# Two early expert tiles: tokens read in 32-token blocks and turned on VectorE, w1 loaded in block order

## The chip, the cores and the metric

One core of one Trainium2 chip runs the whole program. The metric is the device time in microseconds (us). Runs of one kernel on this chip are compared with each other, and the profile is one further execution of the same program.

## The reference

An FFT layer over the sequence is followed by a mixture of experts in which each token goes to one expert.

```python
def _attn_ref(x, w_r, w_i, b_r, b_i):             # x: 8 x 2496 x 256
    X = np.fft.rfft(x, axis=1)
    Yr = Xr @ w_r - Xi @ w_i + b_r                # 256 x 256 each
    Yi = Xr @ w_i + Xi @ w_r + b_i
    ...                                           # soft threshold at 0.01
    y = np.fft.irfft(Y, n=x.shape[1], axis=1)
def _moe_ref(x, w_gate, w1, w2):                  # 19968 tokens, 8 experts
    logits = x @ w_gate
    expert_idx = np.argmax(logits, axis=1)
    ...                                           # gate_w: softmax value of the chosen expert
    for e in range(E):
        mask = expert_idx == e
        h = np.maximum(xe @ w1[e], 0.0)           # 256 -> 1024
        ye = h @ w2[e]                            # 1024 -> 256
        out[mask] = gate_w[mask, None] * ye
```

## The kernel before

**Two phases.** The first (`spectral`) does the transforms of the eight sequences. `route` then works out for each half of a sequence, (b, 0) and (b, 1), in which row of a DRAM table `xs` each token belongs, and its `scatter` writes the tokens there, sorted by expert: up to 11 indirect DMAs a half, issued by GpSimd (POOL) on L813, 117 rows of 264 floats each. The second phase takes `xs` in tiles of 512 tokens of one expert. Tiles 0 to 2 (`EARLY` = 3) begin before the last sequence is scattered, because full tiles of the earlier sequences stand already; tile 3 and all later ones need every scatter. The last 32 scatters, of (6, 1), (7, 0) and (7, 1), run while tiles 0 and 1 are worked on.

**One tile.** `load` reads its tokens, `weights` its expert's w1 and w2. `upright` makes the token matrix with features on the partitions, as a rounded part `xh` (ScalarE, ACT) and a remainder `xl` (VectorE, DVE); `split1` and `split2` cut w1 and w2 in the same way. `up` is the first product, eight groups of six matmuls into a bank `ph`; of each group ACT makes `hh` (L1229) and DVE `hl` (L1230). `down` is the second product, four banks (128 tokens each) of 17 matmuls (L1405, L1406); product j of a bank needs `hh[j]` and `hl[j-1]`. `done` scales the result and sends it to `out` by an indirect DMA (L1269). While `down(t)` runs, its `work` makes the weights and, for tiles 1 and 2, the tokens of tile t+1; tokens of tile 3 and later are made during `up(t)`.

**Two forms of the tokens.** Tiles 0 to 2 are read as rows (`xw`, L1000, one DMA, 1056 bytes a token), and TensorE (PE) turns them by eight 128x128 transposes into `px` (L1172). Tile 3 and later are read in blocks of 32 tokens (`xq`, L1005, four DMAs of 256-byte runs, and `xr`, L1008, two words a token), and DVE turns them by two block transposes (L1148) into `xf`. That leaves the features in another order, so `by_block` loads w1 in the same order (four DMAs of 32 partitions each).

**What sets the order.** PE, SyncE (SP), ACT and DVE run their instructions as the code writes them. POOL's order is made by the compiler's scheduler until `experts_rest`. A scatter may not be moved ahead of the last `mark` copy written before it (`pace`, `gated`): tiny POOL copies (L742) of a word that another engine has just made. `up` of an early tile writes one mark for each `hh` group and two scatters behind it. Any scatter that stands behind the reads of `xs` for tiles 1 and 2 waits until those DMAs are done, since the table's rows could overlap. SP issues all loads in one queue: after the w1 of tile 3 come `xq` and `xr` of tile 3 (which wait for all scatters), the raw w1 `qb` of an expert (L1072, `read_units`; `sum_units` on POOL, L1077 to L1080, and `split_units` on ACT and DVE make a combined form of it that later tiles use), `xq` and `xr` of tile 4, and w2 of tile 3. In `down(2)` ACT and DVE work in this order: `split_units`, `split2(3)`, `split1(3)`; `up(3)` needs the last of these.

Of the kernel before, what the change touches and what calls it, by code (L numbers as in the profile page):

```python
# [10 lines left out]
F32 = mybir.dt.float32  # L11
F32R = mybir.dt.float32r
BF16 = mybir.dt.bfloat16
I32 = mybir.dt.int32
# [10 lines left out]
D = 256  # L25
E = 8
F = 1024
LAM = 0.01
XW = 264
# [8 lines left out]
EARLY = 3  # L38
# [81 lines left out]
class Kernel:  # L120
# [48 lines left out]
    def open_inverse(self, st):  # L169
        nc, nb = self.nc, self.nb  # L170
        cp = self.cp
        self.idle = cp.tile([128, 512], BF16, name="idle")
        nc.vector.memset(self.idle, 0.0)
        self.ident = cp.tile([128, 128], F32, name="ident")
        make_identity(nc, self.ident)
        self.carry = cp.tile([117, E], F32, name="carry")
        self.carry_b = cp.tile([117, E], BF16, name="carry_b")
        self.base = cp.tile([128, E], F32, name="base")
        nc.vector.memset(self.carry, 0.0)
        nc.vector.memset(self.carry_b, 0.0)  # L180
        self.ones_b = cp.tile([117, 128], BF16, name="ones_b")
        nc.vector.memset(self.ones_b, 1.0)
        self.used = cp.tile([128, E], F32, name="used")
        nc.vector.memset(self.used, 0.0)
        self.tabs = [cp.tile([4, 128], I32, name=f"tab{i}") for i in range(4)]
        cp.tile([1, 384 * (len(self.tabs))], I32, name="gap")
        self.drop = cp.tile([128, 128, 2], I32, name="drop")
        self.tcol = cp.tile([128, 6], F32, name="tcol")

        k = self.k = self.pool(st, "k", 1)  # L190
        self.wi = self.pool(st, "wi", 3)
        self.rt = self.pool(st, "rt", 1)
        self.psi = self.pool(st, "psi", 2, space=PSUM)
        self.iw = k.tile([128, 2, 136], F32, name="iw")
        self.gar = k.tile([120, 117], F32, name="gar")
        self.gh = k.tile([120, 117], F32R, name="gh")
        self.gl = k.tile([120, 117], F32R, name="gl")
        self.ids = k.tile([117, nb, G], I32, name="ids")
        self.score = k.tile([117, G, E], F32, name="score")
        self.ltri_f = k.tile([117, 117], F32, name="ltri_f")  # L200
        self.ltri = k.tile([117, 117], BF16, name="ltri")
        self.scan = [k.tile([117, 8 + GH, E], F32, name=f"scan{i}") for i in range(3)]
        for t in self.scan:
            nc.vector.memset(t[:, 0:8, :], 0.0)
        self.mark = k.tile([1, 1], F32, name="mark")
        self.z = k.tile([128, 2, 66, 40], F32, name="z")
# [780 lines left out]
    def load(self, t):  # L987
        if t >= self.nt or t in self.seen:
            return
        self.seen.add(t)  # L990
        nc = self.nc
        n = self.length(t)
        row = self.word(2, t, E * self.cap + 2 * TT - n)
        rows = self.xs[bass.ds(row, n), :]
        if t < self.early:
            if t:
                xr = self.w2p.tile([128, 4, XW], F32, tag="xw", name="xw", bufs=EARLY - 1)
            else:
                xr = self.rt.tile([128, 4, XW], F32, name="xw0")
            nc.sync.dma_start(xr, rows.rearrange("(h p) c -> p h c", h=4))  # L1000
            self.xfs[t], self.xrs[t] = xr, xr[:, :, HEAD:HEAD + 2]
            return
        xq = self.hb.tile([128, 16, 2, 32], F32, tag="xq", name="xq", bufs=2)[:, :n // 32]
        for q in range(4):
            nc.sync.dma_start(xq[32 * q:32 * q + 32].rearrange("p t c i -> p t (c i)"),  # L1005
                              rows[:, 64 * q + q // 2 * E:64 * q + q // 2 * E + 64].rearrange("(t j) c -> j t c", t=n // 32))
        xr = self.hb.tile([128, 4, 2], F32, tag="xr", name="xr", bufs=7)
        nc.sync.dma_start(xr[:, :n // 128, :], rows[:, HEAD:HEAD + 2].rearrange("(h p) c -> p h c", h=n // 128))  # L1008
        self.xqs[t], self.xrs[t] = xq, xr

    def weights(self, t, which):
        if t >= self.nt:
            return
        nc = self.nc
        e = self.word(0, t, E - 1)
        back = 2 if self.wide < t < self.main else 1
        ask = {} if t > self.wide and t - back < self.wide or t == self.main else self.unless_kept(t, back)
        raw1, raw2 = self.raws(t)
        if which == 2:
            parts = [(raw2[q], self.w2[bass.ds(e, 1), q * 512:(q + 1) * 512, :].rearrange("o (c p) f -> p (o c) f", p=128))  # L1020
                     for q in range(2)]
        elif t < self.early:
            parts = [(raw1[:, q], self.w1[bass.ds(e, 1), q * 128:(q + 1) * 128, :].rearrange("o p f -> p (o f)"))
                     for q in range(2)]
        else:
            parts = [(raw1[at], src) for at, src in self.by_block(bass.ds(e, 1))]
        for dst, src in parts:
            nc.sync.dma_start(dst, src, **ask)
# [107 lines left out]
        self.next_weights(t, 2)  # L1136

    def turn_tokens(self, t):
        if t >= self.nt or t < self.early or t in self.xfs:
            return  # L1140
        nc = self.nc
        n = self.length(t)
        xf = self.xf.rearrange("p (c t j) -> p c t j", c=2, t=16)[:, :, :n // 32, :]
        self.xfs[t] = [xf[:, c].rearrange("p t j -> p (t j)") for c in range(2)]
        xq = self.xqs.pop(t)
        for lo in range(0, n // 32, 8):
            hi = min(lo + 8, n // 32)
            nc.vector.transpose(xf[:, :, lo:hi, :].rearrange("p c t j -> p t c j"), xq[:, lo:hi])  # L1148
            yield
# [12 lines left out]
    def upright(self, t):  # L1162
        if t >= self.nt:
            return
        nc = self.nc
        n = self.length(t)
        if t < self.early:
            xf = []
            for c in range(2):
                p = self.psi.tile([128, 512], F32, tag="u", name="px", bufs=4)  # L1170
                for h in range(4):
                    nc.tensor.transpose(p[:, h * 128:(h + 1) * 128], self.xfs[t][:, h, c * 136:c * 136 + 128],  # L1172
                                        self.ident)
                xf.append(p)
        else:
            yield from self.turn_tokens(t)
            xf = self.xfs.pop(t)
        if self.fewer(t) or self.home(t) is self.w2p:
            xh, xl = (self.w2p.tile([128, 2, 2 * TT], F32R, tag=nm, name=nm)[:, :, :n] for nm in ("xh2", "xl2"))
        else:  # L1180
            xh, xl = (self.alt[:, i:i + 4 * TT].rearrange("p (c n) -> p c n", c=2)[:, :, :n] for i in (0, 4 * TT))
        if self.fewer(t):
            sums = self.xsum
            th, tl = self.xss[t] = [self.alt[:, i:i + 3 * TT] for i in (0, 3 * TT)]
        for c in (1, 0) if self.fewer(t) else (0, 1):
            with self.tc.high_priority():
                nc.scalar.copy(xh[:, c], xf[c])
            with self.tc.high_priority():
                nc.vector.tensor_sub(xl[:, c], xf[c], xh[:, c])
            yield  # L1190
        if self.fewer(t):
            nc.scalar.copy(th, sums)
            nc.vector.tensor_sub(tl, sums, th)
            yield
        self.xts[t] = (xh, xl)
# [327 lines left out]
    def experts_rest(self, late):  # L1523
        late.enter_context(self.tc.manual_schedule(engines={mybir.EngineType.Activation, mybir.EngineType.DVE, mybir.EngineType.Pool}))
        self.hb = self.pool(late, "hb", 1)
        self.rt = self.pool(late, "rt2", 1)
        self.xf = self.hb.tile([128, F], F32, name="xf")
        self.xsum = self.hb.tile([128, 3 * TT], F32, name="xsum")
        self.alt = self.hb.tile([128, 8 * TT], F32R, name="alt")
        self.five = self.hb.tile([128, 2 * TT], F32, name="five")  # L1530
# [55 lines left out]
```

## Time and profile before

| what | value |
|---|---|
| median of 3 runs | 1457.04 us (1456.46 to 1457.08) |
| the profiled execution: time | 1456.64 us |
| the profiled execution: span of the core | 1454.8 us |
| busy share PE / DVE / ACT / POOL | 99% / 77% / 67% / 47% |

The span runs from the core's first to its last instruction; 1.8 us of the profiled execution lie outside it. All times below count from the start of the span. Tiles 0 to 3 take up about 563 to 655 us of it.

### The profile page before, as it was taken

What the parts mean: (1) busy time and instruction counts of PE and PEld (TensorE: products, weight loads), DVE (VectorE), ACT (ScalarE), POOL (GpSimd) and SP (SyncE); (2) the same over time, 40 slices, a digit from 0 to 9 for tenths busy, and PEclk for the clock granted to TensorE, in tenths of its full rate; (3) what the DMA queues carried; (4) which work ended last, traced back from release to release, by engine and by line L of the source; (5) the groups of instructions that cost most, each with busy time, mean ns of one, the idle gap of its engine ahead of it and who ended that gap; (6) DMA issues with size and microseconds to landing.
All of it is one profiled execution on the core that took longest, in us unless ns stands there. A gap on an engine that the chain in (4) does not pass through costs nothing.

```text
span 1454.8 us, 30914 instructions
## 1 busy us (share of the span) xinstructions
PE 1436.6 (99%) x9989; PEld 1307.9 (90%) x9990; DVE 1113.5 (77%) x2475; ACT 972.3 (67%) x2054; POOL 683.2 (47%) x791
## 2 busy tenths in 40 slices
PE   9999999999999999999999999999999999999997
PEld 8898989898999988888888899999999999999996
DVE  5778787878888988787787677777777777777785
ACT  5767767677676666566665666666676677666664
POOL 2113342516161536654544566565656655665521
PEclk9999999999999999999999999999999999999999
DMA  7665464646463225699698674273283392751482
GB/s 225 179 203 156 142 189 122 194 122 193 117 191 98 82 90 183 148 250 270 180 242 232 180 213 111 59 233 84 59 254 70 73 241 72 206 129 45 126 239 62
DMA packets 200701, 227.89 MB, mean 157 GB/s; under 512 B 115735, under 2 KB 162213, under 8 KB 195412
## 3 DMA queue, kind: packets, MB, share of 16 engines
q1 hardware_dynamic: 180166, 179.37, 46.3%
q0 software_dynamic: 20144, 46.38, 10.1%
q8 instruction: 81, 1.33, 0.4%
q14 instruction: 89, 0.72, 0.2%
q10 hardware_dynamic: 221, 0.09, 0.0%
HBM read 221.32 MB, written 80.72 MB: 208 GB/s over the span
## 4 chain that ended last, share of the span: by engine, by line
PE 87%; DVE 6%; issue 3%; ACT 2%; POOL 1%; SPq 0%; DMA 0%; DVEq 0%; POOLq 0%; ACTq 0%
PE po L1406 15%; PE pd L1297 10%; PE ph L1225 8%; PE ph L1297 8%; PE po L1405 8%; PE pm L457 6%; PE pz L548 5%; PE pd L1406 5%; PE pb L424 4%; PE pa L381 4%; PE py L562 4%; PE pk L457 3%; PE pv L528 3%; PE pd L1405 2%; DVE y L518 2%
## 5 line engine op out<-in xcount | busy, mean ns | idle before, releaser
L1406 PE MATMUL po<-h,hh 128*128 128x512 f32 x928 | 326.2, 395 | 0.0
L1405 PE MATMUL po<-h,hl 128*128 128x256 f32 x928 | 241.3, 280 | 0.0
L1269 POOL DMA_INDIRECT out<-o,row x80 | 116.7, 1459 | 246.3 <-DVE o L1267 178.4
L813 POOL DMA_INDIRECT xs_dram<-yb,pos x171 | 173.5, 1014 | 62.4 <-issue 31.4
L1406 PEld LDWEIGHTS po<-h,hh 128*128 128x128 f32 x928 | 168.8, 188 | 27.1
L1405 PEld LDWEIGHTS po<-h,hl 128*128 128x128 f32 x928 | 175.0, 189 | 8.7
L518 DVE SCALAR_TENSOR_TENSOR y<-v,r 64x256 f32<-64x256 f32 x320 | 134.0, 419 | 6.4 <-ACT r L505 0.8
L1135 POOL TENSOR_TENSOR h<-r,h 128x512 fp32r<-128x512 f32 x108 | 136.6, 1301 | 0.4
L1406 PE MATMUL pd<-h,hh 128*128 128x512 f32 x368 | 127.8, 394 | 0.0
L1269 POOL DMA_INDIRECT out<-o,xr x70 | 70.8, 1011 | 119.0 <-DVE o L1267 87.4
L742 POOL COPY mark<-v 1x1 f32<-1x1 f32 x70 | 13.7, 196 | 216.1 <-DVE v L491 192.2
L1267 DVE SCALAR_TENSOR_TENSOR o<-po,xr,part 128x256 f32<-128x256 f32 x108 | 51.8, 480 | 82.2 <-ACT part L1266 82.1
L1337 ACT ACTIVATE hh<-pd 128x512 fp32r<-128x512 f32 x108 | 64.6, 598 | 73.3 <-DVE ph L1332 61.3
L1229 ACT ACTIVATE hh<-ph 128x512 fp32r<-128x512 f32 x108 | 64.5, 598 | 69.8 <-PE ph L1225 68.5
L1106 DVE TENSOR_TENSOR l<-r,h 128x512 fp32r<-128x512 f32 x164 | 105.6, 685 | 2.8 <-ACT h L1105 2.2
L1230 DVE SCALAR_TENSOR_TENSOR hl<-ph,hh 128x512 fp32r<-128x512 f32 x108 | 74.1, 689 | 41.7 <-ACT hh L1229 39.2
L1342 DVE SCALAR_TENSOR_TENSOR hl<-pd,hh 128x512 fp32r<-128x512 f32 x108 | 74.6, 691 | 38.4 <-ACT hh L1337 34.4
L1405 PE MATMUL pd<-h,hl 128*128 128x256 f32 x368 | 95.6, 280 | 0.0
L1297 PE MATMUL pd<-alt,qb 128*128 128x256 f32 x648 | 93.6, 280 | 0.8 <-DVE pd L1328 0.8
L548 PE MATMUL pz<-iw,z 128*120 128x136 f32 x684 | 93.6, 279 | 0.3 <-ACT z L532 0.3
L1105 ACT CAST h<-r 128x512 fp32r<-128x512 f32 x164 | 92.9, 617 | 0.0
L528 PEld LDWEIGHTS pv<-bi,y 128*128 128x128 f32 x640 | 79.8, 192 | 13.8 <-issue 7.3
(261 smaller groups left out, 4544.4 us busy)
## 6 DMA issues: line engine op xcount, KB each, us to landing
qb<-pw_dram SPq DMA_DIRECT2D x54, 1024.0 KB
r<-moe_w SPq DMA_DIRECT2D x88, 512.0 KB
r<-moe_w SPq DMA_DIRECT2D x152, 256.0 KB
spec_dram<-ae SPq DMA_DIRECT2D x77, 240.0 KB
t<-spec_dram SPq DMA_DIRECT2D x140, 128.0 KB
xq<-xs_dram SPq DMA_DIRECT2D x140, 128.0 KB
pw_dram<-qb SPq DMA_DIRECT2D x16, 1024.0 KB
x<-x SPq DMA_DIRECT2D x35, 384.0 KB
```

The source lines that it names most:

```text
L457: nc.tensor.matmul(to, a[:, c, slot, :], ww[nm][:, c, :], start=first and i == 0, stop=last and i == 5, skip_group_check=held)
L518: self.nc.vector.scalar_tensor_tensor(out=y[q * 64:q * 64 + 64, kp, :], in0=u[h, q, :], scalar=LAM, in1=r[h, q, :], op0=ALU.add, op1=ALU.min)
L528: nc.tensor.matmul(p[:, c, :, kp, :], y[:, kp, c * 128:(c + 1) * 128], self.bi[:, 2 * s + kp, :], start=True, stop=True)
L548: nc.tensor.matmul(p[:120, c * 128:c * 128 + 136], self.z[:, c, 3 * g:3 * g + 3, :].rearrange("p j a -> p (j a)"), self.iw[:, c, :], start ...
L813: i = nc.gpsimd.indirect_dma_start(out=self.xs[:, :], out_offset=bass.IndirectOffsetOnAxis(ap=pos[:m, g:g + 1], axis=0), in_=y[:m, g, 0:XW ...
L1106: nc.vector.tensor_sub(lo[:, c, s], v, hi[:, c, s])
L1135: self.nc.gpsimd.tensor_sub(lo[:, s, :], self.r2[q // 2][:, q % 2 * 2:q % 2 * 2 + 2, :], hi[:, s, :])
L1225: nc.tensor.matmul(p[:, i, :], a, v[:, c, :], start=m == 0, stop=m == 5)
L1269: i = nc.gpsimd.indirect_dma_start(out=self.out[:, :], out_offset=bass.IndirectOffsetOnAxis(ap=at[h], axis=0), in_=o[:, h, :], in_offset=N ...
L1297: nc.tensor.matmul(to[:, k * TT:k * TT + TT], w, v, start=start and k == m == 0, stop=m == 2, skip_group_check=True)
L1405: nc.tensor.matmul(p[:, :D], hl[:, f, hs], w2[:, f, 0, :], start=False, stop=False)
L1406: nc.tensor.matmul(p, hh[:, j, hs], w2[:, j].rearrange("p a d -> p (a d)"), start=j == 0, stop=j == 7)
```

## The change

Tiles 1 and 2 are read, turned and multiplied as the later tiles are: five DMAs instead of one for the tokens, two DVE block transposes instead of eight PE transposes, w1 in the order of blocks. Tile 0 keeps its old form. The load of w1 of tile 1 loses its condition. The turned tokens `xf` move to a pool that lives from the start, into what had been an unused gap; nothing else in memory moves.

```diff
-        cp.tile([1, 384 * (len(self.tabs))], I32, name="gap")
+        self.xf = cp.tile([128, F], F32, name="xf")
+        cp.tile([1, 384 * (len(self.tabs)) - F], I32, name="gap")
...
-        if t < self.early:
-            if t:
-                xr = self.w2p.tile([128, 4, XW], F32, tag="xw", name="xw", bufs=EARLY - 1)
-            else:
-                xr = self.rt.tile([128, 4, XW], F32, name="xw0")
+        if t == 0:
+            xr = self.rt.tile([128, 4, XW], F32, name="xw0")
             nc.sync.dma_start(xr, rows.rearrange("(h p) c -> p h c", h=4))
...
-        xq = self.hb.tile([128, 16, 2, 32], F32, tag="xq", name="xq", bufs=2)[:, :n // 32]
+        if t < self.early:
+            both = self.w2p.tile([128, 4 * XW], F32, tag="xw", name="xw", bufs=EARLY - 1)
+            xq = both[:, :4 * D].rearrange("p (t c i) -> p t c i", t=16, c=2)
+            xr = both[:, 4 * D:4 * D + 8].rearrange("p (h c) -> p h c", h=4)
+        else:
...
-        ask = {} if t > self.wide and ... else self.unless_kept(t, back)
+        ask = {} if t == which == 1 or t > self.wide and ... else self.unless_kept(t, back)
...
-        elif t < self.early:
+        elif t == 0:
             parts = [(raw1[:, q], self.w1[bass.ds(e, 1), q * 128:(q + 1) * 128, :].rearrange("o p f -> p (o f)"))
...
-        if t >= self.nt or t < self.early or t in self.xfs:
+        if t >= self.nt or t == 0 or t in self.xfs:
...
-        if t < self.early:
+        if t == 0:
             xf = []
```

The order of instructions moves on POOL, about the last 32 scatters. The rows begin where sequence 7 ends (the marks on `y` and `yb`) and tile 0 starts; `xs_dram<-yb,pos` is a scatter, `mark<-hh` a mark on a group of tile 0's `up`, `out<-o` a result of tile 0. Before:

```order
L742 COPY mark<-y 1x1
L742 COPY mark<-yb 1x1
L813 DMA xs_dram<-yb,pos 162304x264 x11
L742 COPY mark<-hh 1x1
L813 DMA xs_dram<-yb,pos 162304x264 x2
...
L742 COPY mark<-hh 1x1
L813 DMA xs_dram<-yb,pos 162304x264 x2
L1269 DMA out<-o,xw_7790 19968x256
L813 DMA xs_dram<-yb,pos 162304x264 x4
```

Now:

```order
L743 COPY mark<-y 1x1
L743 COPY mark<-yb 1x1
L743 COPY mark<-hh 1x1 x6
L814 DMA xs_dram<-yb,pos 162304x264 x23
L1272 DMA out<-o,xw_7791 19968x256
L814 DMA xs_dram<-yb,pos 162304x264 x4
```

Before, eleven scatters stood ahead of the first mark on `hh`, and two behind each of the six marks; now all six marks stand ahead of all 23 scatters. The sixth mark reads group 5 of tile 0's `up`. Behind these rows the order is the same in both: the result DMAs of tile 0 among the last nine scatters, then tile 1's four, then `sum_units`.

On DVE the place is `down(0)`, where the tokens of tile 1 are made; `o` is a result, `xl` the remainder, `pfa` and the rows below it work on a table of tile starts. Before:

```order
L1267 SCALAR_TENSOR_TENSOR o<-po,xw_7790,part 128x256
L1189 TENSOR_TENSOR xl_8981<-px,xh_8980 128x512 x2
L870 COPY pfa<-pfb 128x2
L871 TENSOR_TENSOR pfa<-pfb 128x6
L870 COPY pfb<-pfa 128x4
```

Now:

```order
L1270 SCALAR_TENSOR_TENSOR o<-po,xw_7791,part 128x256
L1151 STREAM_TRANSPOSE xf<-xw 128x8x2x32 x2
L871 COPY pfa<-pfb 128x2
L872 TENSOR_TENSOR pfa<-pfb 128x6
L871 COPY pfb<-pfa 128x4
...
L1270 SCALAR_TENSOR_TENSOR o<-po,xw_7791,part 128x256
L1192 TENSOR_TENSOR xl_9015<-xf,xh_9014 128x512 x2
```

The two transposes stand where `xl` stood, and `xl` moves behind the next result; at tile 2 it is the same.

## Rows read from the trace of the kernel before

**Rows 1.** The page: busy time, share, instructions; the scatters (count, busy, mean ns).

```profile
PE 1436.6 (99%) x9989; PEld 1307.9 (90%) x9990; DVE 1113.5 (77%) x2475; ACT 972.3 (67%) x2054; POOL 683.2 (47%) x791
...
L813 POOL DMA_INDIRECT xs_dram<-yb,pos  x171 | 173.5, 1014 | 62.4 <-issue 31.4
```

**Rows 2.** Timeline of PE about both `px` (start, us, line, [idle before]).

```profile
582.44 1.03 PE L1172 MATMUL px<-ident,xw 128*128 128x128 f32 x8
583.23 0.48 PE L1406 MATMUL po<-h,hh 128*128 128x512 f32 x1
...
606.16 1.03 PE L1172 MATMUL px<-ident,xw 128*128 128x128 f32 x8
```

**Rows 3.** Timeline of DVE, tokens of tiles 1 (`px`) and 3 (`xq`).

```profile
583.75 1.29 DVE L1189 TENSOR_TENSOR xl<-px,xh 128x512 fp32r<-128x512 f32 x2 [2.35 <-ACT xh L1187]
...
618.07 0.70 DVE L1148 STREAM_TRANSPOSE xf<-xq 128x512 f32<-128x512 f32 x1
618.82 0.69 DVE L1230 SCALAR_TENSOR_TENSOR hl<-ph,hh 128x512 fp32r<-128x512 f32 x1
```

**Rows 4.** Timeline of POOL, the last 32 scatters: first, eleventh, last.

```profile
553.49 0.17 POOL L742 COPY mark<-yb 1x1 f32<-1x1 f32 x1 [12.12 <-ACT yb L563]
554.46 1.07 POOL L813 DMA_INDIRECT xs_dram<-yb,pos  x1 [0.80 <-DVE yb L767]
...
567.50 0.99 POOL L813 DMA_INDIRECT xs_dram<-yb,pos  x1 [0.30 <-DVE mx L771]
...
603.12 0.95 POOL L813 DMA_INDIRECT xs_dram<-yb,pos  x1 [0.18 <-issue]
```

**Rows 5.** Timeline of ACT, group 5 of `up(0)`.

```profile
571.27 0.60 ACT L1229 ACTIVATE hh<-ph 128x512 fp32r<-128x512 f32 x1 [0.76 <-PE ph L1225]
```

**Rows 6.** Timeline of SP's DMA issues: `xw` of tiles 1, 2; `xq` of tile 3; `qb`.

```profile
545.09 1.55 SPq L1000 DMA_DIRECT2D xw<-xs_dram  x2
...
607.02 2.00 SPq L1005 DMA_DIRECT2D xq<-xs_dram  x4
...
610.49 1.95 SPq L1072 DMA_DIRECT2D qb<-moe_w  x4
```

**Rows 7.** Waits of SP's queue, 500 to 660 us: total, times, longest.

```profile
SPq L1005 <- DMA xs_dram<-yb,pos: 0.7, 1, 0.7
```

**Rows 8.** Timeline of POOL, `sum_units(2)`, first and third step.

```profile
619.80 1.30 POOL L1077 TENSOR_TENSOR qb<-qb 128x512 f32<-128x512 f32 x1 [7.54 <-DMA qb<-moe_w]
...
622.89 1.62 POOL L1079 TENSOR_TENSOR qb<-qb 128x512 f32<-128x512 f32 x1
```

**Rows 9.** Timeline of ACT, `split_units(2)` begins.

```profile
624.54 1.14 ACT L1086 CAST qb<-qb 128x512 fp32r<-128x512 f32 x2 [2.52 <-POOL qb L1079]
```

**Rows 10.** Timeline of PE, `down(2)` and the start of `up(3)`.

```profile
622.45 0.39 PE L1406 MATMUL pd<-h,hh 128*128 128x512 f32 x1
622.68 0.28 PE L1405 MATMUL pd<-h,hl 128*128 128x256 f32 x1
...
631.84 0.39 PE L1225 MATMUL ph<-alt,h 128*128 128x512 f32 x1
632.26 0.50 PE L1225 MATMUL ph<-alt,l 128*128 128x512 f32 x1
```

**Rows 11.** DMA view, packets of 608 to 609, 609 to 610, 619 to 620 us.

```profile
DMA packets 81, 0.25 MB, mean 254 GB/s; under 512 B 19, under 2 KB 19, under 8 KB 81
...
DMA packets 568, 0.28 MB, mean 278 GB/s; under 512 B 531, under 2 KB 531, under 8 KB 568
...
DMA packets 685, 0.17 MB, mean 171 GB/s; under 512 B 685, under 2 KB 685, under 8 KB 685
```

**Rows 12.** Windows: length, busy PE, PEld, DVE, ACT, POOL, granted clock, DMA, GB/s.

```profile
1444.00:1446.00 2.00, 0.09 (x1) 0.00 (x0) 0.48 (x1) 0.47 (x1) 0.60 (x1) 1.00 0.11 30
...
1448.00:1450.00 2.00, 0.00 (x0) 0.00 (x0) 0.00 (x0) 0.00 (x0) 0.00 (x0) 0.55 0.02 4
```

**Rows 13.** Timeline of PE, the kernel's first eight matmuls.

```profile
1.20 3.44 PE L700 MATMUL pw<-idle 128*128 128x512 bf16 x8 [1.20 <-DVE idle L173]
```

More of the change, by code (lines that the diff above doesn't have):

```diff
@@ L1002, in load @@
             return
-        xq = self.hb.tile([128, 16, 2, 32], F32, tag="xq", name="xq", bufs=2)[:, :n // 32]
+        if t < self.early:
[3 more added lines that the diff above has]
+        else:
+            xq = self.hb.tile([128, 16, 2, 32], F32, tag="xq", name="xq", bufs=2)[:, :n // 32]
+            xr = self.hb.tile([128, 4, 2], F32, tag="xr", name="xr", bufs=7)
         for q in range(4):
@@ L1006, in load @@
                               rows[:, 64 * q + q // 2 * E:64 * q + q // 2 * E + 64].rearrange("(t j) c -> j t c", t=n // 32))
-        xr = self.hb.tile([128, 4, 2], F32, tag="xr", name="xr", bufs=7)
         nc.sync.dma_start(xr[:, :n // 128, :], rows[:, HEAD:HEAD + 2].rearrange("(h p) c -> p h c", h=n // 128))
@@ L1016, in weights @@
         back = 2 if self.wide < t < self.main else 1
-        ask = {} if t > self.wide and t - back < self.wide or t == self.main else self.unless_kept(t, back)
+        ask = {} if t == which == 1 or t > self.wide and t - back < self.wide or t == self.main else self.unless_kept(t, back)
         raw1, raw2 = self.raws(t)
@@ L1526, in experts_rest @@
         self.rt = self.pool(late, "rt2", 1)
-        self.xf = self.hb.tile([128, F], F32, name="xf")
+        self.hb.tile([128, F], F32, name="space3")
         self.xsum = self.hb.tile([128, 3 * TT], F32, name="xsum")
```

## The prediction

> **What bounds the kernel now.** I read the busy shares first. PE works for 1436.6 of 1454.8 us, 99% [rows 1], so a microsecond taken from PE is worth one, as long as nothing that feeds PE comes later. The reader is to see in that line that PE has no reserve, while DVE and POOL have. The change touches tiles 1 and 2, so I read next the timelines of PE and DVE where their tokens are made. The eight transposes of tile 1 start at 582.44 and the product behind them at 583.23: they take 0.79 us of PE [rows 2]. DVE stood idle 2.35 us there, because it waited for what came out of them [rows 3].
>
> Then I followed what else stands behind the reads that change. The order of POOL moves, so I read POOL's timeline over the last 32 scatters: the first starts at 554.46, the eleventh at 567.50, the last at 603.12 [rows 4]. The queue of SP shows who waits for the last one: the tokens of tile 3 are asked for at 607.02, after 0.7 us in which the queue had nothing to wait for but a scatter [rows 6, 7]. So the last scatter's start is followed 607.02 - 603.12 = 3.9 us later by that load, with no slack between them.
>
> Two things hang on that point of SP's queue. The tokens of tile 3 were turned at 618.07 with no idle time ahead [rows 3]; they had some slack. The raw w1 `qb`, issued next, had none: POOL waited 7.54 us for it and began `sum_units(2)` at 619.80 [rows 8], ACT waited 2.52 us for POOL's third step and began `split_units(2)` at 624.54 [rows 9], and behind that, in the same queues, lie `split2(3)` and `split1(3)`. At the end PE shows it: the first matmul of `up(3)` starts at 631.84 and the second, which needs the remainder of w1, at 632.26. That is a step of 0.42 us where the two matmuls at 622.45 and 622.68 stand 0.23 apart [rows 10]. PE was already waiting for this chain, a little, so what delays the chain delays PE.
>
> **The change part by part.** *PE.* 16 transposes go: 2 x 0.79 = 1.58 us less [rows 2], the second time at 606.16.
>
> *DVE and ACT.* Four block transposes are added, 0.70 us each by that of tile 3, two for each tile [rows 3]. They start right after a result, without waiting for PE, in the idle time of 2.35 us, and PE has the fourth bank of `down` before it needs them (9.16 us pass from 622.68, in the first bank of tile 2, to `up` at 631.84, so a bank is about 2.8 us [rows 10]). `xl` moves behind the third result, still within that bank. I cost this at nothing; if the cover were gone, it would be 1.4 us a tile.
>
> *The loads.* Ten DMAs stand for two. They are issued from 545.09 [rows 6] and first needed by DVE after 580, so their smaller packets cost nothing here. w1 of tile 1 needs all of tile 0's to be split before its first DMA, where two halves went one by one; it is first used in `down(0)`, after 574, some 20 us later. Nothing either.
>
> *POOL.* This is the term that decides. The first of the 32 scatters waits for these loads in both kernels, but now it also stands behind six marks, and the sixth needs group 5 of `up(0)`, which ACT ends at 571.27 + 0.60 = 571.87 [rows 5]. With about 0.4 us for the mark and the next start, the first scatter goes at 572.3 and not at 554.46, 17.8 us later. From first to last took 48.66 us, four results and eight marks among them. Six marks leave the stretch. They hardly shorten it, for a scatter starts 0.18 us after a mark [rows 4] where it otherwise starts some 0.3 us after a scatter. The shortest that I can find is the pace of the first eleven, 13.04 / 10 = 1.304 us, over 35 steps: 45.6 us. The longest is the 48.66 itself. I take 48.2, since only marks go. The last scatter then starts at 620.5, 17.4 us later (bounds 14.8 and 17.9).
>
> *SP.* The tokens of tile 3 are asked for 3.9 us after that, at 624.4. The queue behind is the same, so every load in it moves: `xq` (four DMAs) and `xr` of tile 3, `qb` (four), `xq` and `xr` of tile 4, w2 of tile 3.
>
> *From there to POOL's sums* took 619.80 - 607.02 = 12.78 us. Part of it was a backlog: between 608 and 609 the queues still moved 62 packets of 4 KB (w1 of tile 3) and 19 small ones, and only from 609 to 610 come the 256-byte packets of the tokens, 531 of them [rows 11], up to 2.4 us after the issue. In the new place w1 of tile 3 has long landed, so this part shrinks, by nothing at least and by 2.4 us at most. I take 1.6, since some time between issue and first packet stays. The sums then start at 624.4 + 11.2 = 635.6, 15.8 us later.
>
> *From the sums to `up(3)`* nothing changes in kind: the same casts and subtractions in the same queues. w2 of tile 3 comes in between and is also late, but it is asked for no later against the sums than now. So the second matmul of `up(3)` moves from 632.26 to about 648.1, +15.8 us. The 1.58 us gained on PE come before this wait and vanish in it. Behind it the queues have the distances that they have now, and I see nothing that gives the time back.
>
> *The clock.* PE will stand still for some 10 us in `down(2)` (from about 621 to 631: `hl` of group 5, and all behind it, stands on DVE behind the late transposes of tile 3). After PE's last matmul, which ends at about 1444.1, the granted clock is still 1.00 up to 1446 and 0.55 on average from 1448 to 1450 [rows 12], so it fell from 2.4 to 1.2 GHz within about 4 us. At half rate the first eight matmuls took 3.44 us, 0.43 each [rows 13], against 0.23 at full rate: 1.6 us lost at a restart. The restart inside `down(2)` is hidden, since PE would finish the banks some 4 us before `up(3)` can go. The pause after that is too short, by rows 12, to lower the clock again. So I add nothing. The Trainium skill, TensorE: Matmul & The Clock Gate, Part 1, says that the half rate is the default state and that activity releases it, so each pause would have its price. By that rule taken for both pauses the result would be 1.6 us later, 1474.4; the trace agrees that the clock falls after the last matmul, and no row here shows a fall after a pause within the work.
>
> *Sum.* The profiled execution took 1456.64 us, 1.84 more than its span, and the median of the runs is 0.40 above it. 1456.64 + 15.8 = 1472.4; on the median, 1457.04 + 15.8 = 1472.8.
>
> **The rivals.**
>
> *Only the tokens of tile 3 bind.* If the chain through `qb` had slack that I do not see, the stall would be that of the tokens alone. They are asked for at 624.4; 2048 packets at 685 per us [rows 11] are 3.0 us; with start and landing I estimate 6 us, so 630.4. DVE then needs two transposes and three `hl` (about 0.7 each [rows 3]) and waits a little for ACT: 634.4. PE has 8.6 of the 9.16 us left, so `up(3)` starts at 643.0 against 631.84: +11.2, 1468.2. For it: the tokens had slack and `qb` is a longer way. Against it: the three waits of rows 8 to 10.
>
> *The pauses cost clock, or late loads pile up.* `up(3)` begins at half rate (+1.6, +3.2 if twice), or w2 of tile 3 arrives behind the sums: 1474.4 to 1477.5. For it: the fall in rows 12. Against it: PE's pause ahead of `up(3)` is under 4 us.
>
> *Faster: the scatters lose nothing.* If POOL reached the scatters as early as now, only PE's 1.58 us would count: 1455.5. It decides from the point at which the sixth mark is passed: at 554.5 nothing is lost, and at 556.0 the delay has eaten the gain, for `qb` has no slack. Against it: `hh` of group 5 is not there before 571.87 [rows 5], and POOL runs its rows in their order. For it: only that I may misjudge what the marks wait for.
>
> *No change.* The gain and the loss would have to cancel, with the sixth mark at 556; I see no mechanism.
>
> **How the numbers follow.** 0.2% of this kernel, 2.9 us, is about what a measurement of it can tell from no change. Forecast, +13 to +18: 0.72. Tokens alone, about +11: 0.08. Clock or pile-up, +17.4 to +20.5: 0.15. Faster: 0.04; the same: 0.01. So faster 0.04, same 0.01, slower 0.95. The likeliest gives 1472.8 us. The bounds of the unknown costs are 14.8 - 2.4 = 12.4 and 17.9 - 0 = 17.9, that is 1469.4 to 1474.9. The range reaches a little into the tokens' case below and to the end of the clock's above: 1467.5 to 1477.5.
>
> **What the profile of the changed kernel would show.** Right: POOL idle from about 554 to 572, then 23 scatters in a row; the last scatter at about 620; `xq` of tile 3 at about 624; DVE idle ahead of the transposes of tile 3 until about 630; PE idle by some 10 us in `down(2)` and again ahead of `up(3)`, which starts near 647; between tile 1 and that point PE 1.6 us ahead of now; after it, all stages as long as now. Wrong: scatters from about 555 on, or a first wait of PE at another place, or a granted clock of 0.50 in `up(3)`.

## The result, and the profile of the changed kernel

The changed kernel takes 1474.18 us (median of 4 runs, 1473.71 to 1474.64), the kernel before beside it 1456.75 us: ratio 1.0119, 95% interval 1.0107 to 1.0131. It is slower by 17.4 us, where 15.8 were forecast. The profiled execution took 1473.71 us with a span of 1471.9.

POOL's timeline shows the term that decided (start, us, engine, line, work, idle before and what ended it). It answers to rows 4, 5 and 8: six marks first, and the last of them waits for ACT; then the scatters in one row.

```profile
566.48 0.17 POOL L743 COPY mark<-hh 1x1 f32<-1x1 f32 x1 [12.32 <-ACT hh L1232]
...
572.51 0.17 POOL L743 COPY mark<-hh 1x1 f32<-1x1 f32 x1 [0.87 <-ACT hh L1232]
573.74 0.99 POOL L814 DMA_INDIRECT xs_dram<-yb,pos  x1 [1.06 <-DMA r<-moe_w]
...
618.33 0.17 POOL L743 COPY mark<-hh 1x1 f32<-1x1 f32 x1
...
620.99 0.18 POOL L743 COPY mark<-hh 1x1 f32<-1x1 f32 x1
621.34 0.94 POOL L814 DMA_INDIRECT xs_dram<-yb,pos  x1 [0.18 <-issue]
...
636.00 1.30 POOL L1080 TENSOR_TENSOR qb<-qb 128x512 f32<-128x512 f32 x1 [8.12 <-DMA qb<-moe_w]
```

SP's queue, the counterpart of rows 6: the ten reads of tiles 1 and 2 are spread over 545.58 to 556.45, where two took 1.55 us. The tokens of tile 3 are asked for 3.3 us after the last scatter, `qb` 2.6 us after them.

```profile
545.58 4.13 SPq L1009 DMA_DIRECT2D xw<-xs_dram  x4
549.89 2.33 SPq L1011 DMA_DIRECT2D xw<-xs_dram  x1
553.02 2.85 SPq L1009 DMA_DIRECT2D xw<-xs_dram  x4
556.06 0.39 SPq L1011 DMA_DIRECT2D xw<-xs_dram  x1
...
624.64 1.94 SPq L1009 DMA_DIRECT2D xq<-xs_dram  x4
...
627.22 1.99 SPq L1075 DMA_DIRECT2D qb<-moe_w  x4
```

PE's timeline, for rows 2 and 10: it has no wait of note from `up(0)` to the fifth of the eight groups of `up(2)`; then it stands for long twice, ahead of that group and ahead of `up(3)`, and for 0.46 us in between, at 634.10.

```profile
563.41 0.40 PE L1228 MATMUL ph<-xh,h 128*128 128x512 f32 x1
...
608.51 0.40 PE L1228 MATMUL ph<-xh,h 128*128 128x512 f32 x1
...
622.57 0.80 PE L1228 MATMUL ph<-xh,h 128*128 128x512 f32 x1 [8.44 <-DVE hl L1233]
...
647.00 0.80 PE L1228 MATMUL ph<-alt,h 128*128 128x512 f32 x1 [3.94 <-ACT h L1108]
647.89 0.79 PE L1228 MATMUL ph<-alt,l 128*128 128x512 f32 x1
...
661.11 0.40 PE L1409 MATMUL pd<-h,hh 128*128 128x512 f32 x1
```

The same points in the trace of before, where PE has no such wait: `up(0)`, `up(2)` and `down(3)` begin.

```profile
562.89 0.40 PE L1225 MATMUL ph<-xh,h 128*128 128x512 f32 x1
...
609.81 0.40 PE L1225 MATMUL ph<-xh,h 128*128 128x512 f32 x1
...
643.63 0.39 PE L1406 MATMUL pd<-h,hh 128*128 128x512 f32 x1
```

The first of these waits is not in the prediction. The waits between 500 and 665 us (engine, line, what it waited for: us, times, longest) name it: ACT's first `hh` of `up(2)` may not overwrite the buffer until POOL has made its marks on the `hh` of `up(1)`, and these two marks (618.33 and 620.99) stand behind nearly all scatters. `hl` on DVE waits for that `hh`, PE for a bank that `hl` frees.

```profile
DVE hl L1233 <- ACT hh L1232: 18.2, 9, 12.1
...
ACT hh L1232 <- POOL mark L743: 12.0, 1, 12.0
```

The windows view (us, busy PE, PEld, DVE, ACT, POOL, granted clock, DMA, GB/s) shows what the second pause leaves behind: PE goes on at 0.50, which is 1.2 GHz, after a pause of 3.9 us.

```profile
642.00:646.00 4.00, 1.07 (x7) 0.67 (x5) 3.98 (x9) 3.06 (x8) 1.19 (x1) 0.98 1.02 199
646.00:650.00 4.00, 2.90 (x6) 2.01 (x7) 4.00 (x8) 3.24 (x7) 2.47 (x2) 0.50 0.72 209
650.00:654.00 4.00, 4.00 (x13) 3.13 (x13) 1.58 (x4) 1.19 (x2) 1.92 (x2) 0.67 1.04 307
```

Where the time went: `down(3)` starts at 661.11, and at 643.63 in the trace of before, 17.48 us later; the spans differ by 17.1, so all of it is lost before that point, and only 0.4 us comes back behind it. The second matmul of `up(3)` is 647.89 - 632.26 = 15.63 later (0.52 of it is already there when `up(0)` starts, 563.41 against 562.89). From there to `down(3)` it takes 13.22 us where before took 643.63 - 632.26 = 11.37: 1.85 more, in the stretch that runs at half clock.

### The profile page after: what moved, and what is told of

The parts are those of the page before. It is cut to its first block, busy times and chain, and to the rows that moved or that the text cites. A ratio compares the mean times of both kernels' runs of the same rounds, so it can differ in the third digit from the quotient of the medians.

```text
span 1471.9 us, 30925 instructions
## 1 busy us (share of the span) xinstructions
PE 1440.9 (98%) x9974; PEld 1310.0 (89%) x9974; DVE 1114.7 (76%) x2479; ACT 972.2 (66%) x2054; POOL 681.0 (46%) x791
## 4 chain that ended last, share of the span: by engine, by line
PE 83%; DVE 6%; issue 4%; ACT 2%; DMA 2%; POOL 1%; SPq 1%; DVEq 0%; ACTq 0%; POOLq 0%
PE po L1409 14%; PE pd L1300 10%; PE ph L1300 8%; PE ph L1228 7%; PE po L1408 7%; PE pm L458 6%; PE pz L549 5%; PE pd L1409 5%; PE pb L425 4%; PE pa L382 4%; PE py L563 4%; PE pk L458 3%; PE pv L529 3%; PE pd L1408 2%; DVE y L519 2%
```

## The experiments

**Three sets of runs.** Eight of the twelve runs fell into two sets in which the kernel before itself takes 1494.8 and 1495.2 us and single runs lie up to 7 us from the median. What they tell stands at the end; the four that follow are one set in which the kernel before took 1456.98 us. What makes the difference between the levels was not found: the chip is numbered 1 in the first of the two sets and 10 in the second, and 1 also in the set at 1457 us, so nothing here shows that the level belongs to a chip. The changed kernel was run in none of the three. It stood beside a kernel before of 1456.75 us, so its time can be set against the set at 1457 us directly, and against the others not at all.

**1. Scatters ahead of the marks again.** The changed kernel with one more rule for the scheduler: a mark may not be moved ahead of a scatter that was written before it. POOL's order is then that of before, but for the mark on `yb`, which now stands behind ten of the scatters.

```diff
             self.paced = self.nc.gpsimd.tensor_copy(self.mark, after)
+            if self.sent is not None:
+                self.tc.add_manual_dep(self.paced.ins, self.sent.ins.name, ..., reason="scatters first")
...
                 self.behind_mark(i)
+                self.sent = i
```

> The first run of the first set again, scatters ahead of the marks, beside these: 11 to 14 us less than the changed kernel, and 0 to 4.5 us more than the kernel before, by how far the ten reads still hold the first scatter.

Measured: 1461.56 us, ratio 1.0032 (1.0020 to 1.0044): 12.6 us less than the changed kernel, 4.6 more than the kernel before. POOL, then PE, whose first line has its counterpart in before at 560.39:

```profile
561.75 1.00 POOL L817 DMA_INDIRECT xs_dram<-yb,pos  x1 [18.20 <-DVE zl L555]
...
610.33 1.39 POOL L817 DMA_INDIRECT xs_dram<-yb,pos  x1 [0.19 <-issue]
...
625.52 1.29 POOL L1084 TENSOR_TENSOR qb<-qb 128x512 f32<-128x512 f32 x1 [8.64 <-DMA qb<-moe_w]
```

```profile
562.61 1.04 PE L1179 MATMUL px<-ident,xw 128*128 128x128 f32 x8
...
635.93 0.50 PE L1232 MATMUL ph<-alt,h 128*128 128x512 f32 x1 [1.96 <-ACT h L1112]
637.30 0.50 PE L1232 MATMUL ph<-alt,l 128*128 128x512 f32 x1 [0.87 <-DVE l L1113]
...
648.66 0.39 PE L1413 MATMUL pd<-h,hh 128*128 128x512 f32 x1
```

The order of POOL alone gives 12.6 of the 17.4 us back: 10.59 of it ahead of the second matmul of `up(3)`, and 1.86 behind it, where the stage now takes 11.36 us and not 13.22. What is left, 5.04 us at that matmul, is of two kinds. Tile 0's transposes start 2.2 us later than in before. Of this shift 0.97 is there at 16 us and 2.08 at 94 us, where PE waits once for a DMA (`t<-spec_dram`, 0.77 us at 91.80), and up to 550 us POOL runs its rows in the order of before; so the order of the scatters doesn't make it, and whether other executions have it stays open. The other 2.8 us come from the first scatter, which is 7.3 us later than in rows 4, 5.1 without the shift, though no mark on `hh` stands ahead of it. The profile puts its wait down to DVE's `zl`, which a scatter doesn't read. The ten reads explain it better: their packets fill the stretch up to 560 us, by the DMA view of 559 to 560 and 560 to 561.

```profile
DMA packets 589, 0.06 MB, mean 63 GB/s; under 512 B 581, under 2 KB 581, under 8 KB 589
...
DMA packets 47, 0.17 MB, mean 172 GB/s; under 512 B 5, under 2 KB 5, under 8 KB 47
```

A comparison among the runs of section 5 fits this. With the tokens read by one DMA a tile, the first scatter follows the mark on `yb` by 0.79 us (0.80 in rows 4); with ten reads and no marks on `hh` at all, it follows that mark by 7.50 us:

```profile
573.83 1.07 POOL L814 DMA_INDIRECT xs_dram<-yb,pos  x1 [0.79 <-DVE yb L768]
```

```profile
578.39 0.99 POOL L814 DMA_INDIRECT xs_dram<-yb,pos  x1 [7.50 <-DMA r<-moe_w]
```

In the changed kernel the packets end at about 558 us, so there such a wait would be hidden behind the marks.

**2. The second pause filled.** Sixteen matmuls that nothing reads, into the bank that `up(3)` takes first.

```diff
         for f2 in range(8 // per):
...
+            if t == 3 and f2 == 0:
+                for _ in range(16):
+                    self.nc.tensor.matmul(p[:, 0, :], self.idle[:, 0:128], self.idle, start=True, stop=True)
```

> The changed kernel, with 16 more matmuls that nothing reads, into the bank that up(3) takes first, placed between down(2) and up(3), so that PE works through most of the 3.9 us in which it waits there. Theory (the pause ahead of up(3) halves the granted clock, and the restart costs some 1.9 us): the granted clock of up(3) stays at 1.00, its first matmul still starts when the chain through qb is done, and the time falls by 1.5 to 2 us against the changed kernel. Rival (the stage is slow for another reason, late w1 or w2): no gain.

Measured: 1472.87 us, ratio 1.0112 (1.0096 to 1.0127). The interval overlaps that of the changed kernel, so the time alone doesn't settle it; the profile does. PE (the row has 15 of the 16), then windows:

```profile
643.19 3.63 PE L1224 MATMUL ph<-idle 128*128 128x512 bf16 x15
647.40 0.50 PE L1231 MATMUL ph<-alt,h 128*128 128x512 f32 x1 [0.59 <-ACT h L1108]
648.29 0.50 PE L1231 MATMUL ph<-alt,l 128*128 128x512 f32 x1 [0.39 <-DVE l L1109]
...
659.66 0.39 PE L1412 MATMUL pd<-h,hh 128*128 128x512 f32 x1
```

```profile
646.00:650.00 4.00, 2.99 (x11) 1.49 (x10) 3.66 (x7) 3.65 (x8) 1.97 (x2) 1.00 0.68 196
```

The granted clock stays at 1.00, and from the second matmul to `down(3)` it takes 659.66 - 648.29 = 11.37 us, exactly as in before, where the changed kernel takes 13.22. So the half clock behind the pause costs 1.85 us. At `down(3)` this run is 1.45 us ahead of the changed kernel, as the chain through `qb` was 0.4 us later here; the medians differ by 1.3.

**3. `qb` ahead of the tokens.** In the changed kernel, `read_units` is written before `load` of tile 3; POOL keeps its late order.

```diff
-        self.load(self.early)
         parts = iter(range(E))
...
         self.read_units(self.early - 1)
+        self.load(self.early)
```

> The changed kernel, with the raw w1 qb asked for ahead of the tokens of tile 3 in SP's queue; POOL's order stays as late as it is. Theory (qb's chain is what up(3) waits for, the late tokens and hh of tile 2 hold down(2) a little less): sum_units(2) starts behind the results of tile 1 at about 628 and not 636; up(3) starts when PE is through down(2), about 643, or up to 1 us later with w2 of tile 3; the pause is too short for the clock to fall: 4 to 6 us less than the changed kernel. Rival (w2 of tile 3, late in SP's queue, is what binds): no gain. Rival (only qb's chain was late, tokens and hh were not): 12 us less.

Measured: 1466.67 us, ratio 1.0069 (1.0054 to 1.0084), 7.5 us less than the changed kernel; 4 to 6 were expected. POOL begins the sums right behind the results of tile 1, and PE enters `up(3)` without a wait:

```profile
626.31 0.98 POOL L1272 DMA_INDIRECT out<-o,xw  x1 [0.30 <-DVE h L1126]
627.31 1.31 POOL L1080 TENSOR_TENSOR qb<-qb 128x512 f32<-128x512 f32 x1
```

```profile
642.51 0.39 PE L1409 MATMUL pd<-h,hh 128*128 128x512 f32 x1
642.74 0.40 PE L1228 MATMUL ph<-alt,h 128*128 128x512 f32 x1
...
653.94 0.40 PE L1409 MATMUL pd<-h,hh 128*128 128x512 f32 x1
```

`up(3)` starts 4.26 us earlier and takes 11.20 us, not 14.11: the `qb` chain was the wait that ended last. Taken away, what is left is the wait for the marks (8.46 us, in `up(2)`) and for the late tokens (`hl` in `down(2)`, 0.46 and 1.59):

```profile
622.01 0.80 PE L1228 MATMUL ph<-xh,h 128*128 128x512 f32 x1 [8.46 <-DVE hl L1233]
...
633.93 0.39 PE L1408 MATMUL pd<-h,hl 128*128 128x256 f32 x1 [1.59 <-DVE hl L1233]
```

My expectation fell short since I gave the clock 1.9 us and forgot that the stage also waits 0.9 us for its second matmul.

**4. No marks on `hh` in `up(1)`.** The wait that the prediction didn't have is taken away with what causes it.

```diff
-                self.pace(hh.bitcast(F32)[0:1, f2, 0:1])
+                if t == 0:
+                    self.pace(hh.bitcast(F32)[0:1, f2, 0:1])
```

> The changed kernel without the two marks on hh in up(1), so that ACT's first hh of up(2) has no late reader of the old hh to wait for. Theory (this wait of 12 us ends before others that come later): up(2) runs at once, PE then waits in down(2) behind the late transposes of tile 3, as the prediction had it, and up(3) starts no earlier: within 0.7 us of the changed kernel. Rival (this wait is what carries the loss): 8 to 12 us less.

Measured: 1470.77 us, ratio 1.0097 (1.0082 to 1.0113): 3.4 us less, where I had expected no more than 0.7. PE:

```profile
629.82 0.58 PE L1409 MATMUL pd<-h,hl 128*128 128x256 f32 x1 [8.04 <-DVE hl L1233]
...
644.84 0.49 PE L1228 MATMUL ph<-alt,h 128*128 128x512 f32 x1 [1.20 <-ACT h L1108]
645.73 0.50 PE L1228 MATMUL ph<-alt,l 128*128 128x512 f32 x1 [0.40 <-DVE l L1109]
...
657.10 0.39 PE L1410 MATMUL pd<-h,hh 128*128 128x512 f32 x1
```

The pause moves to `down(2)`, where the prediction had it, with nearly the same length. The gain has another source: without the marks, the scheduler puts the last scatter at 620.19, one result earlier, and the tokens of tile 3 go at 622.73, 1.9 us sooner; the second matmul of `up(3)` is 2.2 us sooner. And the pause ahead of `up(3)` is down to 1.20 us, after which the stage runs at full clock: 645.73 to 657.10, where `down(3)` starts, is 11.37 us. 2.2 and 1.85 make 4.0, of which the median shows 3.4. By this account the wait added nothing of its own to the loss; the run changes POOL's order along with it, so this is worked out and not shown apart.

**5. The two sets at 1495 us.** Six versions ran there, two of them twice. First the reverse of experiment 1: the kernel before, its scatters held behind the sixth mark.

```diff
+            if six:
+                for i in self.sent[-21:]:
+                    self.gated(i)
...
-                self.pace(hh.bitcast(F32)[0:1, f2, 0:1])
+                self.pace(hh.bitcast(F32)[0:1, f2, 0:1], six=t == 0 and f2 == 5)
```

> The kernel before, with the one difference that its last 23 early scatters may not go ahead of the sixth mark on hh, which gives POOL the order of the changed kernel; reads, PE transposes and w1 stay as they were. Theory (the order alone carries the loss): first scatter near 572.5, last near 620.5, hh of up(2) waits some 12 us for the mark in tile 1, up(3) goes at about 647 and starts at half clock: 1473.5 to 1475 us, as the changed kernel, since PE's 1.6 us vanish in the wait. Rival (the reads or the block transposes carry a part): clearly less, 1457 to 1470.

> The kernel before with its last 23 early scatters behind the sixth mark on hh, as the changed kernel has them, and nothing else changed. Theory (the order alone carries the loss): first scatter near 572.5, up(3) at about 647 and at half clock: 1472.5 to 1475 us. Rival (the reads and the block transposes carry a part of it that the order alone does not): 1457 to 1470.

Measured: 1505.15 us, ratio 1.0059 (1.0039 to 1.0080), and 1505.86 us, 1.0072 (1.0049 to 1.0096). It is slower, as the theory says, by half of what was expected, and not by the theory's mechanism. Here PE itself is late: in the second run it stands for 21.6 us between 590 and 650 with nothing that the profile shows to wait for, and comes to `up(3)` at 682.00 with no wait ahead of it. So these runs do not test the order's price, and the reverse of experiment 1 is still to be made at the level of 1457 us.

```profile
PE po L1410 <- issue: 16.0, 4, 10.1
PE po L1409 <- issue: 5.6, 3, 2.4
```

```profile
682.00 0.40 PE L1229 MATMUL ph<-alt,h 128*128 128x512 f32 x1
```

The changed kernel with the scatters first (experiment 1, first run), then with rows read by one DMA a tile (two runs; this version leaves out the order of the features in tiles 1 and 2, so their results are not the reference's):

> The changed kernel, with the one difference that no mark on POOL may go ahead of a scatter written before it, so that POOL's order is again that of the kernel before. Theory (POOL's order carries the loss, and the reads a small part of it): the first scatter then waits for the reads of tiles 1 and 2 alone; in the changed kernel their small packets flow until about 558, where they ended at about 553 before, so it starts at 559 to 560, some 4.5 us later than before and 14 us earlier than in the changed kernel. The chain through qb is late by 3 to 4.4 us, PE waits that long ahead of up(3), too short for the clock to fall: 1460 to 1461.5 us. Rival (the reads cost nothing for the scatters): 1455.5 to 1457. Rival (the loss lies in the reads, the block transposes or w1, not in the order): 1474 as the changed kernel.

> The changed kernel, with the tokens of tiles 1 and 2 read by one DMA each as rows, as before; the block transposes and w1 in block order stay, so the features of these two tiles' tokens are out of order and their results are not the reference's. POOL's order falls back to that of the kernel before by itself. Theory (the ten reads alone move POOL's order and end later): scatters from 555, qb's chain where it was before, and the second matmul of up(3) at 632.3 plus the 0.5 us by which this trace's times are shifted. If qb's chain is what up(3) waits for, the 1.6 us that PE gains are lost there: 1456.8 us, no change. Rival: PE's gain counts in full, as the prediction's faster case had it: 1455.4. Rival (block transposes or w1 in block order carry the loss): 1465 to 1474.

> The changed kernel with the tokens of tiles 1 and 2 read by one DMA each as rows, which puts the features of these two tiles' tokens out of order; block transposes and w1 in block order stay, and POOL's order is that of the kernel before. Theory (PE's gain is lost at up(3), since qb's chain is where it was): 1456.3 to 1457.2 us. Rival (the gain counts): 1455.4. Rival (the block transposes cost something): over 1458.

```diff
         if t < self.early:
+            xr = self.w2p.tile([128, 4, XW], F32, tag="xw", name="xw", bufs=EARLY - 1)
+            nc.sync.dma_start(xr, rows.rearrange("(h p) c -> p h c", h=4))
+            flat = xr.rearrange("p h c -> p (h c)")
+            self.xqs[t] = flat[:, :4 * D].rearrange("p (t c i) -> p t c i", t=16, c=2)
...
```

Measured: 0.9998 (0.9981 to 1.0014); 1.0004 (0.9989 to 1.0018) and 1.0006 (0.9992 to 1.0019). Both are the same as the kernel before in these sets, where the first was expected some 0.2 to 0.3% above it. What the order of the changed kernel costs at this level is not known. (That a pause of 3 to 4.4 us is too short for the clock to fall, as the first expectation has it, doesn't fit the changed kernel's trace, where it fell in a pause of 3.94.) For the second, one thing doesn't hang on the level: with one read a tile, the scheduler makes POOL's order of before by itself, in the program's listing and in its trace:

```
COPY mark<-yb 1x1
DMA xs_dram<-yb,pos 162304x264 x11
COPY mark<-hh 1x1
DMA xs_dram<-yb,pos 162304x264 x2
```

So of the change's parts it is the ten reads that move POOL's order; the block transposes and the block order of w1 leave it alone.

Last, three attempts at a version that beats both: experiments 1 and 3 together; no mark on `hh` at all, with `qb` first; and the same two mends in the kernel before.

> The changed kernel with POOL's order mended as in the first run of this set, and with the raw w1 qb asked for ahead of the tokens of tile 3 in SP's queue, so that it doesn't wait for the scatters. Theory: qb's chain is no longer what up(3) waits for; the tokens of tile 3 come some 4 us later than before, which they can afford in part; PE's gain of 1.6 us shows: 1455 to 1456.5 us, and no wait ahead of up(3). Rival (w2 of tile 3, behind all this in SP's queue, or the tokens, bind next): 1458 to 1461.

> The changed kernel without any mark on hh, and with the raw w1 qb asked for ahead of the tokens of tile 3. Theory: the first scatter waits for the ten reads alone (about 560 against 554.5), neither ACT nor qb's chain waits for POOL, tokens of tile 3 are asked for near 611 and still come in time; PE waits nowhere from up(0) to up(3) and is 1.6 us ahead of the kernel before: 1455 to 1456 us, less than both kernels. Rival (w2 or the tokens of tile 3 bind next): 1458 or more.

> The kernel before with the same two mends: no mark on hh, qb asked for ahead of the tokens of tile 3; tokens of tiles 1 and 2 turned by PE. Theory (qb's chain held up(3) by 0.2 us only): 1456.5 to 1457 us, and 1.2 to 1.6 us more than the run with the block transposes and the same mends. Rival (the mends are what helps, not the block transposes): the same as that run.

Measured, in that order: 1.0008 (0.9989 to 1.0027), 1.0052 (1.0033 to 1.0071), 1.0029 (1.0016 to 1.0042). The first two were expected below the kernel before and the third level with it; none beats it there, and the last two are slower. In the set at 1457 us they were not run; whether the first of them would gain PE's 1.8 us stays open.

## Why the prediction was right, and where it wasn't

| step | predicted | measured |
|---|---|---|
| first of the 32 scatters | 572.3 | 573.74 |
| last scatter | 620.5 | 621.34 |
| tokens of tile 3 asked for | 624.4 | 624.64 |
| `sum_units(2)` | 635.6 | 636.00 |
| second matmul of `up(3)` | 648.1 | 647.89 |
| from there to `down(3)` | 11.37, as before | 13.22 |
| PE's gain, `up(0)` to `up(2)` | 1.58 | 1.82 |

**POOL and SP.** The chain from the sixth mark to `up(3)` came out within 1.5 us at every step, and within 0.4 from SP on. The start was 1.4 us late: 0.5 is the shift that the trace has from the beginning, and 1.06 us pass between the last mark and the first scatter, where I had put 0.4 for the mark and the start together. That the later steps come out closer is in part luck, since three terms were too long by 0.6 us each and eat the late start: the scatters took 47.60 and not 48.2, SP asked for the tokens 3.30 and not 3.9 after the last one, and from the sums to the second matmul of `up(3)` it took 11.89 and not 12.5. (The upper bound of the last scatter's delay, 17.9, is 17.8 by its own terms; nothing hangs on it.) Experiment 1 shows that the order is what costs, experiment 3 that of the chains behind it the one through `qb` ends last.

**PE.** From `up(0)` to `up(2)` took 608.51 - 563.41 = 45.10 us, and 609.81 - 562.89 = 46.92 before: 1.82 less, and it did vanish in the later wait.

**The place of the first pause** was wrong. I followed the late tokens of tile 3 to `down(2)`, and missed that the late POOL also holds two marks on `hh` of tile 1, whose readers keep ACT from writing `hh` of tile 2. I had asked who waits for the scatters, not who waits for the other instructions queued behind them. By experiment 4 this cost no time, because the tokens then stop PE for as long, but the stage and the cause that I named were not the first to stop PE.

**The clock** is the step that was mis-sized: "The pause after that is too short, by rows 12, to lower the clock again. So I add nothing." Rows 12 show full clock until 1446 and a mean of 0.55 from 1448 on; I took the whole distance as what a pause needs, and it is only how long that one fall took. The trace after has the fall within the work: 0.98 over 642 to 646, 0.50 over 646 to 650. By single us it is 1.00 over 644 to 645, 0.91 over 645 to 646 and 0.50 over 646 to 647, where PE had stopped at 643.07; at the end of the kernel before it is still 1.00 over 1447 to 1448, where PE had stopped at 1444.1. So the term that I put at nothing costs 1.85 us, by experiment 2, and 15.63 + 1.85 = 17.48 is the loss. In number that is the lower end of the rival with clock, 1474.4 us, and 1474.18 were measured. The Trainium skill, TensorE: Matmul & The Clock Gate, Part 1, has it that half rate is the default and activity releases it; the trace agrees, with 0.50 behind the pause and 1.00 again from 653 on. The first pause lowered the clock too (0.57 over 618 to 622), and that was hidden, as forecast, since PE had to wait again. Rows 13 alone do not show half rate, for the granted clock of the first 5 us reads 1.00; the price of 0.43 us a matmul is borne out all the same, for behind the first pause, at 0.50, the matmuls at 623.16 and 623.59 stand 0.43 apart.

**Its own signs of being wrong.** Two of the three that the prediction named were seen: a first wait of PE at another place, and a granted clock of 0.50 in `up(3)`. So the path through POOL and `qb` was right, and the total lies within the range; the account of PE's pauses was not right.

**The reads** "cost nothing": true in the changed kernel, but only under the cover of the marks. The reason that I gave was that DVE needs the tokens late; that the first scatter waits for the reads too I had written, and not priced. With the marks out of the way the scatters are 5.1 us late (experiment 1). By that, POOL's old order alone would not have brought the 1455.5 us of the rival in which the scatters lose nothing: the chain through `qb` would still have been late. And even with the scatters at their old time PE's gain would vanish in the wait; I had that in the sum and not in the rival.

## What to carry to other kernels

When a scheduler orders one engine, compare that order before and after for any edit, even one that names other engines: here ten reads in place of two put six tiny copies ahead of 23 scatters, and that cost 12.6 us where the edit was worth 1.8. Follow every instruction that is queued behind a late one, also those that only read a single-buffered tile, for its next writer waits for them (here 12.0 us on ACT, which another late chain covered). And price a pause of PE like the one ahead of `up(3)` twice: the wait, and the half clock behind it, unless another wait follows that hides it.

## What was not expected of the hardware

In the two sets at 1495 us the whole loss of 38 us lies ahead of 690 us: from 690 to 1400 PE is busy for 709.2 of 710 us in all eight runs, as in the trace of before. About half of it is there before tile 0 begins: its transposes start at 576.17 to 585.19, and at 560.39 in the trace of before. In the stretch of the late scatters PE stands with no releaser in the profile ("issue"), by 21.6 us in the second run of the reversed order and by 8.0 us in the second run with rows read:

```profile
PE ph L1231 <- issue: 8.0, 1, 8.0
```

The three versions in these sets in which the 23 scatters run in one row (ratios 1.0029 to 1.0072) are slower than the kernel before, the three in which marks stand between them (0.9998 to 1.0008) are not; but the stalls are not theirs alone, for the run just shown has marks between them. The changed kernel, at 1474 us, has the same 23 in a row and PE has no such wait. What holds PE there was not found.
